# Linear attention feeding a two-layer block: q times k^T v for two chunks at once, with k^T v as the stationary operand

## The chip, the core and the metric

The kernel runs on one core of a Trainium2 chip, in one launch. The metric is the device time of that core in microseconds. The kernel before takes 947.47 us (median of 3 runs, 946.95 to 947.53).

## What is computed

Everything is in 32-bit floats. The reference, cut to what matters:

```python
# q, k, v: (8 batches, 8 heads, 576 positions, 64)
kv  = einsum('bhsd,bhse->bhde', k, v)          # one 64x64 matrix for each batch and head
out = einsum('bhsd,bhde->bhse', q, kv)
x   = out / sqrt(mean(out * out, axis=-1) + 1e-06) * g_norm
x   = x.transpose(0, 2, 1, 3).reshape(4608, 512)
h   = x @ w_in                                 # 512 -> 2048
g   = s * max(h, 0)**2 + b
y   = g @ w_out                                # 2048 -> 512
```

The 4608 rows are handled as 36 chunks of 128, four to a unit, so there are nine units, u = 0 to 8. The two large products take most of the time; the kernel computes them with sums and differences of blocks in place of some of the products. The change touches the small part in front of them: q times k^T v, the norm, and the turning of x.

## The kernel before

While a unit runs its large products, the attention of the four chunks of the next unit is woven in as side work. Unit 0 and unit 1 do this between the products with `w_out` (`side_of`, by slots). The later units do it between the products with `w_in` (`sides`, with places (s, n), where s is the block of the hidden size, 0 to 3, and n the place within it):

```python
for s in range(NS if u > 0 else 0):
    a = steps[s]
    at(0);  a["x1"]()
    if s:  x3(steps[s - 1])
    a["z2"]();  at(1)
    if s:  y4(steps[s - 1])
    a["x6"]();  at(2)
    a["y7"]()
    # ... cut
    at(3);  a["x5"]()
```

Each of x1, z2, x6, y7, x5, x3, y4 is four matmuls of 256 columns on the full array, and each 32-bit matmul appears in the profile as two records, so such a product is a row of `x8`.

The attention of a chunk, cut to the form of chunks 4 and later:

```python
def turn():                        # q^T: by VectorE in 32x32 blocks (chunks 9 and later)
    st["qT"] = attp.tile([P, NP, P], FP32, name="qT", tag="qT")
    nc.vector.transpose(out=st["qT"], in_=q_in[c])      # earlier chunks: TensorE, then a copy

def product():                     # q^T stationary in 128x32 tiles, k^T v moves
    pool, tag = (ps_f, "y") if c > 16 and c % 2 else (ps_a, "x")
    ps = pool.tile([P, NP, P], FP32, name="x_ps", tag=tag)
    for w in range(4):
        for p in range(NP):        # NP = 4: pairs of heads
            nc.tensor.matmul(ps[32 * p : 32 * p + 32, w, :],
                lhsT=st["qT"][:, p, 32 * w : 32 * w + 32],
                rhs=bd_kv[(b if w < 2 else b1) % 2][:, p, :], start=True, stop=True)
    nc.scalar.activation(st["xn"], st["x"], AF.Square)
# row_sum: VectorE sums; norm: ScalarE root, VectorE reciprocal and scaling;
# turn_x: VectorE turns x in 32x32 blocks, ScalarE scales by g_norm
```

`bd_kv[b % 2]` holds k^T v of batch b, two heads of a pair as the diagonal blocks of a 128x128 matrix. `kv_product(b)` makes it, and it is due in the unit before the first chunk that needs batch b:

```python
kv_due = {(b // 2 * R + b % 2 * 4) // 4 - 1: b for b in range(2, B)}   # {1: 2, 2: 3, 3: 4, ...}
```

In unit 2, `kv_product(3)` stands at (1, 3). Its k and v come through the same ring of seven buffers and the same SyncE queue as the weights (`pump`). In unit 1 that queue also loads q for the first two chunks of unit 3, in eight parts between the pumps (`loads_in_parts(3, 0, 8)` at slots 6 to 13). The places of the side work in unit 2 before:

```python
first = {
    (1, 0): [turn[0]],
    (1, 1): [product[0], row_sum[0]],
    (1, 2): [norm[0]],
    (1, 3): [*kv, turn_x[0]],
    (2, 0): [turn[1]],
    (2, 1): [product[1], row_sum[1]],
    (2, 2): [norm[1], *q[0]],
    (2, 3): [turn_x[1], turn[2]],
    (3, 0): [product[2], row_sum[2]],
    # ... cut
}
second = {3: [product[3]], "sums": [row_sum[3]], "norm": [norm[3]], 4: [turn_x[3]]}
```

Of the kernel before, what the change touches and what calls it, by code (L numbers as in the profile page):

```python
# [16 lines left out]
def kernel(  # L17
# [39 lines left out]
    nc = tc.nc  # L57
# [19 lines left out]
    qp = ctx.enter_context(tc.tile_pool(name="qp", bufs=2))  # L77
    attp = ctx.enter_context(tc.tile_pool(name="attp", bufs=2))
    xp = ctx.enter_context(tc.tile_pool(name="xp", bufs=1))
# [13 lines left out]

    kv_in, q_in, w_raw = {}, {}, {}

# [33 lines left out]
    def load_q(c, queues=(nc.sync, nc.sync)):  # L129

        t = qp.tile([P, 2 * DM], FP32, name="q_sb", tag="q")
        pieces = []
        for i in range(2):
# [259 lines left out]

    def attention(c, first=False):

# [3 lines left out]


        b, b1 = parts(c)[0][0], parts(c)[-1][0]
        st = {}

        def turn():
            st["qT"] = attp.tile([P, NP, P], FP32, name="qT", tag="qT")
            if c >= R:
                nc.vector.transpose(out=st["qT"], in_=q_in[c])
                return  # L410
            if c in (0, 2):
                ps = ps_a.tile([P, NP, P], FP32, name="qT_ps", tag="x")
            elif c == 3:
                ps = bank_of("q", "z", 1).rearrange("p b (m n) -> p (b m) n", m=2)
            else:
                ps = ps_t.tile([P, NP, P], FP32, name="qT_ps", tag="t")
            for p in range(NP):
                nc.tensor.transpose(ps[:, p, :], q_in[c][:, 2 * p : 2 * p + 2, :], ident)
            st["q_ps"] = ps
            if not first:  # L420
                take()

        def take():
            if first and c != 1:
                nc.vector.tensor_copy(out=st["qT"], in_=st["q_ps"])
            else:
                nc.scalar.copy(st["qT"], st["q_ps"])

        def product(with_sum=True):
            if first:  # L430
                ps = bank_of("att", "xy"[c % 2]).rearrange("p b (m n) -> p (b m) n", m=2)
            else:
                pool, tag = (ps_f, "y") if c > 16 and c % 2 else (ps_a, "x")
                ps = pool.tile([P, NP, P], FP32, name="x_ps", tag=tag)
            if c < 2:
                for p in range(NP):
                    matmul(ps[:, p, :], st["qT"][:, p, :], bd_kv[0][:, p, :], True, True)
            for w in range(4 if c >= 2 else 0):
                for p in range(NP):
                    nc.tensor.matmul(  # L440
                        ps[32 * p : 32 * p + 32, w, :],
                        lhsT=st["qT"][:, p, 32 * w : 32 * w + 32],
                        rhs=bd_kv[(b if w < 2 else b1) % 2][:, p, :],
                        start=True,
                        stop=True,
                    )
            st["x"] = ps.rearrange("p c (l d) -> p (c l) d", l=2)
            st["xn"] = attp.tile([P, H, D], FP32, name="xn", tag="xn")
            nc.scalar.activation(st["xn"], st["x"], AF.Square)
            if with_sum:  # L450
                row_sum()

        def row_sum():
            st["ss"] = attp.tile([P, H], FP32, name="ss", tag="ss")
            nc.vector.reduce_sum(st["ss"], st["xn"], axis=mybir.AxisListType.X)

        def norm():
            rms = attp.tile([P, H], FP32, name="rms", tag="rms")
            nc.scalar.activation(rms, st["ss"], AF.Sqrt, bias=eps_col, scale=1.0 / D)
            inv = attp.tile([P, H], FP32, name="inv", tag="inv")  # L460
            nc.vector.reciprocal(inv, rms)
# [10 lines left out]
        def turn_x():  # L472
            u, j = divmod(c, 4)
            if j == 0:
                pool = late["x"] if u > 2 and u % 2 else xp
                xT[u] = pool.tile([P, KC, 2 * TB], FP32, name="xT", tag="xT")
            to = xT[u][:, :, j * P : j * P + P]
# [13 lines left out]
            if j % 2 == 1:  # L491
                to = xT[u][:, :, j * P - P : j * P + P]
                for i in range(KC):
                    nc.scalar.activation(  # L494
                        to[:, i], to[:, i], AF.Copy, scale=g_col[:, i : i + 1]
                    )

        return turn, product, norm, turn_x, take, row_sum

    def whole(product, norm):  # L500
        def run():
            product()
            norm()
        return run

# [664 lines left out]

    turn, product, norm, turn_x, take, _ = zip(*(attention(c, True) for c in range(4)))
    slots0 = [slot for s in range(NS) for slot in mm1_plain(s)]
# [37 lines left out]

    def chunks_of(u):
        return list(zip(*(attention(c) for c in range(4 * u, 4 * u + 4))))

    def side_of(u):

        turn, product, norm, turn_x, *_ = chunks_of(u + 1)
        product = [whole(*steps) for steps in zip(product, norm)]
        side = {
            2: [turn[0]],
            3: [product[0]],  # L1220
            4: [turn[1]],
            5: [turn_x[0], product[1]],
            6: [turn[2]],
            7: [turn_x[1], product[2]],
            8: [turn[3]],
            9: [turn_x[2], product[3]],
            11: [turn_x[3]],
            12: [lambda: [sums() for sums in x_sums(u + 1)]],
        }
        if u == 0:  # L1230
            side = {
                6: [lambda: kv_product(1)],
                7: [turn[0]],
                8: [product[0], turn[1]],
                9: [turn_x[0], product[1], turn[2]],
                10: [turn_x[1], product[2], turn[3]],
                11: [turn_x[2], product[3]],
                12: [turn_x[3], lambda: [sums() for sums in sums_w_in(0)]],
                13: side[12],
            }  # L1240
        if u == 1:
            for n, fn in enumerate(loads_in_parts(3, 0, 8)):
                side.setdefault(6 + n, []).append(fn)
# [44 lines left out]
    def sides(u):  # L1288
# [4 lines left out]
        if u + 1 < U:  # L1293
            turn, product, norm, turn_x, _, row_sum = chunks_of(u + 1)
            product = [partial(fn, False) for fn in product]
        kv = [lambda: kv_product(kv_due[u]), lambda: pump(NP)] if u in kv_due else []
# [6 lines left out]
        if u + 1 == U:  # L1303
            return first, second
        if u == 2:
            first = {
                (1, 0): [turn[0]],
                (1, 1): [product[0], row_sum[0]],
                (1, 2): [norm[0]],
                (1, 3): [*kv, turn_x[0]],  # L1310
                (2, 0): [turn[1]],
                (2, 1): [product[1], row_sum[1]],
                (2, 2): [norm[1], *q[0]],
                (2, 3): [turn_x[1], turn[2]],
                (3, 0): [product[2], row_sum[2]],
                (3, 1): [norm[2]],
                (3, 2): [turn_x[2]],
                (3, 3): [turn[3]],
            }
            second = {3: [product[3]], "sums": [row_sum[3]], "norm": [norm[3]], 4: [turn_x[3]]}  # L1320
            for n, fn in enumerate(loads_in_parts(4, 1, 3)):
                second["q", n] = [fn]
        else:
            first = {
                (0, 1): [turn[0]],
                (0, 3): [turn[1]],
                (1, 1): product[:2],
                (1, 2): row_sum[:2],
                (1, 3): [*kv, *q[0], *norm[:2]],
                (2, 0): turn_x[:2],  # L1330
            }
            if u > 3:
                first[1, 2] = [*turn[2:], *row_sum[:2]]
                first[2, 0] = [*turn_x[:2], *q[1]]
                first.update({
                    (2, 1): product[2:],
                    (2, 2): row_sum[2:],
                    (2, 3): norm[2:],
                    (3, 0): [turn_x[2]],
                    (3, 1): [turn_x[3]],  # L1340
                })
            else:
                first[2, 0] = [*turn_x[:2], turn[2]]
                parts = loads_in_parts(5, 1, 4)
                second["q", 0] = [parts[3]]
                first.update({
                    (2, 1): [product[2]],
                    (2, 2): [turn[3], row_sum[2], norm[2], *parts[:3]],
                    (2, 3): [turn_x[2]],
                    (3, 0): [product[3], row_sum[3]],  # L1350
                    (3, 1): [norm[3]],
                    (3, 2): [turn_x[3]],
                })
        second[5], second[6] = [[lambda n=n: x_sums(u + 1)[n]()] for n in range(2)]
# [93 lines left out]
```

## Time and profile before

| what | value |
|---|---|
| time, median of 3 | 947.47 us |
| span of the profiled execution | 945.3 us |
| TensorE matmul busy | 931.7 us, 99% |
| VectorE busy | 657.1 us, 70% |
| ScalarE busy | 205.0 us, 22% |
| DMA | 165.85 MB, mean 175 GB/s |
| products of q with k^T v (line 440) | 1056 + 32 records |

In the profile PE is TensorE, PEld its loading of the stationary operand, DVE VectorE, ACT ScalarE, POOL GpSimd and SP SyncE. L440 is line 440 of the kernel. In a timeline a row gives its start, its length, engine, line, operation, `written<-read`, the form, and `xN` records merged into it; a bracket at the end is idle time before it and what ended that. A busy TensorE is not TensorE at its peak, since records overlap: what a stretch costs is read from the starts of the rows around it. A wait for several things is put down to the one that came last.

### The profile page before, as it was taken

Reading aid. Unit: us, or ns where it says so; the run is one execution under the profiler, and the core shown is the slowest. Engines: PE = TensorE matmul, PEld = TensorE weight load, DVE = VectorE, ACT = ScalarE, POOL = GpSimd, SP = SyncE. Lnnn points to the kernel's source line nnn. Section 1 sums busy time; section 2 is a strip of 40 time slices with the busy share of each in tenths; the row PEclk is TensorE's granted clock in tenths of the full one; section 3 lists DMA queues with packets and bytes.
Section 4 is the critical chain, followed back from the end, with each engine's and each line's share of the span. In section 5 each row is a group of like instructions: output and inputs, shape, how many; then the busy total and the mean of one; then the engine's idle time right before and its main releaser. Section 6 shows DMA issues by size and latency. Waiting matters only on the chain.

```text
span 945.3 us, 18302 instructions
## 1 busy us (share of the span) xinstructions
PE 931.7 (99%) x7438; PEld 841.4 (89%) x7438; DVE 657.1 (70%) x1220; ACT 205.0 (22%) x387; POOL 87.8 (9%) x170
## 2 busy tenths in 40 slices
PE   7999999999999999999999999999999999999997
PEld 7888888888888998899889988999889988998997
DVE  2789767576567785777577756786678757774585
ACT  2784131111122012310232013201320033001200
POOL 2000011033500020000200030003000200021000
PEclk9999999999999999999999999999999999999999
DMA  9688827468952676257544864378326800681075
GB/s 231 211 314 248 266 79 218 118 208 273 286 161 65 221 231 194 36 180 224 193 112 131 262 196 111 78 248 267 98 46 220 304 16 12 204 291 52 12 233 168
DMA packets 129571, 165.85 MB, mean 175 GB/s; under 512 B 78160, under 2 KB 85072, under 8 KB 129360
## 3 DMA queue, kind: packets, MB, share of 16 engines
q1 hardware_dynamic: 118256, 142.71, 49.7%
q0 software_dynamic: 7488, 19.41, 6.2%
q10 hardware_dynamic: 3744, 2.56, 1.1%
q8 instruction: 59, 0.97, 0.4%
q14 instruction: 24, 0.20, 0.1%
HBM read 136.84 MB, written 27.79 MB: 174 GB/s over the span
## 4 chain that ended last, share of the span: by engine, by line
PE 65%; DVE 2%; ACT 1%; issue 0%
PE x_ps L91 27%; PE y_ps L91 18%; PE t_ps L91 8%; PE z_ps L91 8%; PE x_ps L440 2%; PE kv_ps L377 1%; ACT xT L494 1%; DVE a L637 0%; DVE s L247 0%; DVE a L250 0%; DVE a L551 0%; DVE xT L488 0%; DVE a L247 0%; ACT a L631 0%; ACT r L596 0%
## 5 line engine op out<-in xcount | busy, mean ns | idle before, releaser
L596 ACT COPY r<-x_ps 128x512 f32<-128x512 f32 x96 | 56.0, 584 | 397.5 <-PE x_ps L91 375.9
L91 PE MATMUL y_ps<-xs,wb 128*128 128x256 f32 x512 | 122.7, 382 | 0.3 <-DVE a L247 0.3
L91 PE MATMUL x_ps<-xs,ws 128*128 128x256 f32 x512 | 122.0, 381 | 0.5
L822 POOL DMA_DIRECT2D out_dram<-o x110 | 54.5, 502 | 696.7 <-DVE o L247 537.8
L91 PEld LDWEIGHTS x_ps<-xs,ws 128*128 128x128 f32 x512 | 96.4, 190 | 15.3 <-ACT r L596 2.3
L91 PEld LDWEIGHTS y_ps<-xs,wb 128*128 128x128 f32 x512 | 95.4, 190 | 16.3 <-DVE a L247 2.5
L247 DVE TENSOR_TENSOR a<-y_ps,r 128x512 f32<-128x512 f32 x64 | 43.8, 684 | 76.9 <-ACT r L596 59.9
L91 PE MATMUL x_ps<-xT,wa 128*128 128x256 f32 x384 | 89.8, 380 | 0.1
L91 PEld LDWEIGHTS x_ps<-xT,wa 128*128 128x128 f32 x384 | 72.2, 190 | 10.5 <-ACT xT L494 0.5
L91 PE MATMUL y_ps<-w_sb,sub 128*128 128x128 f32 x560 | 69.5, 275 | 0.1
L91 PEld LDWEIGHTS y_ps<-w_sb,sub 128*128 128x128 f32 x560 | 66.4, 192 | 0.6 <-DVE sub L250 0.3
L551 DVE SCALAR_TENSOR_TENSOR a<-a 128x512 f32<-128x512 f32 x89 | 61.5, 691 | 2.8
L91 PE MATMUL y_ps<-w_sb,a 128*128 128x128 f32 (+1 forms) x416 | 61.1, 295 | 0.0
L91 PE MATMUL x_ps<-xT,ws 128*128 128x256 f32 x256 | 60.5, 379 | 0.0
L91 PE MATMUL z_ps<-xT,wa 128*128 128x256 f32 x256 | 60.5, 379 | 0.0
L91 PE MATMUL x_ps<-w_sb,s 128*128 128x256 f32 x256 | 57.8, 380 | 0.0
L91 PEld LDWEIGHTS y_ps<-w_sb,a 128*128 128x128 f32 x416 | 55.4, 192 | 2.2 <-issue 0.2
L91 PE MATMUL t_ps<-w_sb,sub 128*128 128x128 f32 x448 | 54.8, 275 | 0.0
L91 PEld LDWEIGHTS z_ps<-xT,wa 128*128 128x128 f32 x256 | 48.6, 190 | 6.6
L91 PEld LDWEIGHTS x_ps<-xT,ws 128*128 128x128 f32 x256 | 48.1, 190 | 6.3
L91 PEld LDWEIGHTS x_ps<-w_sb,s 128*128 128x128 f32 x256 | 47.5, 190 | 6.0 <-issue 0.2
L91 PEld LDWEIGHTS t_ps<-w_sb,sub 128*128 128x128 f32 x448 | 52.3, 192 | 0.2
(146 smaller groups left out, 1379.1 us busy)
## 6 DMA issues: line engine op xcount, KB each, us to landing
w_sb<-w SPq DMA_DIRECT2D x154, 512.0 KB, 4.7
w_sb<-w SPq DMA_DIRECT2D x42, 256.0 KB, 3.5
w_raw<-in_moe_w_in_dram SPq DMA_DIRECT2D x8, 1024.0 KB, 7.3
w_raw<-in_moe_w_out_dram SPq DMA_DIRECT2D x8, 1024.0 KB, 4.9
w_sb<-in_k_dram SPq DMA_DIRECT2D x48, 144.0 KB, 3.3
w_sb<-in_v_dram SPq DMA_DIRECT2D x48, 144.0 KB, 3.8
w<-sub POOLq DMA_DIRECT2D x24, 256.0 KB, 5.2
out_dram<-o POOLq DMA_DIRECT2D x92, 64.0 KB, 3.9
```

The source lines that it names most:

```text
L91: nc.tensor.matmul(o, lhsT=lhsT, rhs=rhs, start=start, stop=stop, skip_group_check=True)
L247: nc.vector.tensor_tensor(out=o, in0=a, in1=b, op=ALU.add)
L377: nc.tensor.matmul(ps[r][l * HB : l * HB + HB, i, :], lhsT=kv[l][rows, 0, j, :], rhs=kv[l][rows, 1, j, :], start=(j == 0), stop=(j == R - 1),)
L440: nc.tensor.matmul(ps[32 * p : 32 * p + 32, w, :], lhsT=st["qT"][:, p, 32 * w : 32 * w + 32], rhs=bd_kv[(b if w < 2 else b1) % 2][:, p, :] ...
L494: nc.scalar.activation(to[:, i], to[:, i], AF.Copy, scale=g_col[:, i : i + 1])
L551: nc.vector.scalar_tensor_tensor(t, t, 0.0, t, ALU.max, ALU.mult)
L596: nc.scalar.copy(st[name], src)
L822: queues[s % 2].dma_start(out=view[b, jj, :, cols], in_=st[name, j][s * w : s * w + w, cols])
```

## The change

From chunk 4 on, two chunks (256 rows of x) are handled together. k^T v becomes the stationary operand, in tiles of 64 rows by 32 columns, and q^T moves past it, 256 columns in one matmul. This swaps the roles of the operands: fewer stationary loads, longer moves, and eight tiles in place of four. The result arrives turned, so VectorE turns it back in 32x32 blocks, out of PSUM into the tile that held q. Where the 256 rows belong to two batches, the columns are split in two runs. The norm's steps work on both chunks at once.

```diff
-    attp = ctx.enter_context(tc.tile_pool(name="attp", bufs=2))
+    attp = ctx.enter_context(tc.tile_pool(name="attp", bufs=1))
...
+    def attention_of_two(c):
+        ...
+        def turn(i=None):          # one VectorE transpose of both chunks' q
+            ...
+        def product():
+            ps = [ps_t.tile([P, 2, 2 * P], FP32, name="y_ps", tag="t") for _ in range(2)]
+            for b, lo, hi in runs:
+                for r in range(2):
+                    for p in range(NP):
+                        for l in range(2):
+                            rows = slice(l * HB, l * HB + HB)
+                            at = l * HB + r * 32
+                            nc.tensor.matmul(
+                                ps[l][32 * p : 32 * p + 32, r, lo:hi],
+                                lhsT=bd_kv[b % 2][rows, p, at : at + 32],
+                                rhs=st["qT"][rows, p, lo:hi],
+                                start=True, stop=True)
+            st["y"] = q_tile[c].rearrange("p (w l d) -> p w l d", w=W, l=2)
+            for l in range(2):
+                nc.vector.transpose(
+                    out=st["y"][:, :, l].rearrange("p w (r e) -> p r w e", r=2),
+                    in_=ps[l].rearrange("p r (w t) -> p r w t", w=W))
+        def square():   # ScalarE, 1024 elements out of SBUF
+        def row_sum():  # VectorE sum, ScalarE root
+        def norm():     # VectorE reciprocal and scaling
+        def turn_x():   # VectorE
```

The places change as well. All of `first` and `second` for units 2 to 7 is replaced by one list (A is the pair of the first two chunks, B that of the others):

```diff
+        soon = u == 2
+        first = {
+            (0, 1): [A["turn"], *(kv if soon else [])],
+            (0, 3): [A["product"]],
+            (1, 0): [A["square"]],
+            (1, 1): [*([] if soon else kv), A["row_sum"]],
+            (1, 2): [A["norm"], B["turn"]],
+            (1, 3): q[0],
+            (2, 0): [A["turn_x"], A["scale"]],
+            (2, 1): [B["product"]],
+            (2, 2): [B["square"]],
+            (2, 3): [B["row_sum"]],
+            (3, 0): [B["norm"]],
+            (3, 1): [B["turn_x"], *q[1]],
+            (3, 2): [B["scale"]],
+        }
```

In units 0 and 1 the four chunks' steps in `side_of` become two pairs' steps at slots 2 to 12. Loads and `pump` keep their places in unit 1; in unit 2 and later all q loads stand at (1, 3) and (3, 1).

More of the change, by code (lines that the diff above doesn't have):

```diff
@@ L91, in matmul @@
         nc.tensor.matmul(o, lhsT=lhsT, rhs=rhs, start=start, stop=stop, skip_group_check=True)
-    kv_in, q_in, w_raw = {}, {}, {}
+    kv_in, q_in, q_tile, w_raw = {}, {}, {}, {}
     def load_kv(b, i, pool, queues=(nc.sync, nc.sync), **kw):
@@ L133, in load_q @@
         t = qp.tile([P, 2 * DM], FP32, name="q_sb", tag="q")
+        q_tile[c] = t
         pieces = []
@@ L394, with half_of, small, attention @@
     late, xT = {}, {}
-    def attention(c, first=False):
-        b, b1 = parts(c)[0][0], parts(c)[-1][0]
+    two_of = {}
+    def half_of(name, c):
+        if c % 2 == 0:
+            two_of[name] = attp.tile([P, 2 * DM], FP32, name=name, tag=name)
+        t = two_of[name]
+        if name == "qT":
+            return t.rearrange("p (a x) -> p a x", a=NP)[:, :, c % 2 * P : c % 2 * P + P]
+        return t[:, c % 2 * DM : c % 2 * DM + DM].rearrange("p (h d) -> p h d", h=H)
+    def small(name, n, i=""):
+        return attp.tile([P, n], FP32, name=name, tag=f"{name}{i}")
+    def attention(c):
         st = {}
         def turn():
[L407 to L410, printed above, removed]
+            st["qT"] = half_of("qT", c)
             if c in (0, 2):
@@ L419, in turn @@
             st["q_ps"] = ps
-            if not first:
-                take()
         def take():
-            if first and c != 1:
+            if c != 1:
                 nc.vector.tensor_copy(out=st["qT"], in_=st["q_ps"])
@@ L427, in take @@
                 nc.scalar.copy(st["qT"], st["q_ps"])
[L429 to L434, printed above, removed]
+        def product():
+            ps = bank_of("att", "xy"[c % 2]).rearrange("p b (m n) -> p (b m) n", m=2)
             if c < 2:
@@ L442, in product @@
                         lhsT=st["qT"][:, p, 32 * w : 32 * w + 32],
-                        rhs=bd_kv[(b if w < 2 else b1) % 2][:, p, :],
+                        rhs=bd_kv[0][:, p, :],
                         start=True,
@@ L447, in product @@
             st["x"] = ps.rearrange("p c (l d) -> p (c l) d", l=2)
-            st["xn"] = attp.tile([P, H, D], FP32, name="xn", tag="xn")
+            st["xn"] = half_of("xn", c)
             nc.scalar.activation(st["xn"], st["x"], AF.Square)
[L450 to L454, printed above, removed]
+            st["ss"] = small("ss", H, c % 2)
             nc.vector.reduce_sum(st["ss"], st["xn"], axis=mybir.AxisListType.X)
         def norm():
-            rms = attp.tile([P, H], FP32, name="rms", tag="rms")
+            rms = small("rms", H, c % 2)
             nc.scalar.activation(rms, st["ss"], AF.Sqrt, bias=eps_col, scale=1.0 / D)
-            inv = attp.tile([P, H], FP32, name="inv", tag="inv")
+            inv = small("inv", H, c % 2)
             nc.vector.reciprocal(inv, rms)
@@ L474, in turn_x @@
             if j == 0:
-                pool = late["x"] if u > 2 and u % 2 else xp
-                xT[u] = pool.tile([P, KC, 2 * TB], FP32, name="xT", tag="xT")
+                xT[u] = xp.tile([P, KC, 2 * TB], FP32, name="xT", tag="xT")
             to = xT[u][:, :, j * P : j * P + P]
@@ L491, in turn_x @@
             if j % 2 == 1:
[L492 to L504, printed above, removed]
+                scale_x(u, j - 1)
+        return turn, product, norm, turn_x, take
@@ new lines, in scale_x @@
+    def scale_x(u, j):
+        to = xT[u][:, :, j * P : j * P + 2 * P]
+        for i in range(KC):
+            nc.scalar.activation(to[:, i], to[:, i], AF.Copy, scale=g_col[:, i : i + 1])
+    def attention_of_two(c):
+        u, j = divmod(c, 4)
+        by_block = []
+        for i in range(2):
+            p = parts(c + i)
+            by_block += [p[0][0]] * 2 + [p[-1][0]] * 2
+        runs = []
+        for w, b in enumerate(by_block):
+            if runs and runs[-1][0] == b:
+                runs[-1][2] = 32 * w + 32
+            else:
+                runs.append([b, 32 * w, 32 * w + 32])
+        W = 8
+        st = {}
+        def turn(i=None):
+            if i in (None, 0):
+                st["qT"] = attp.tile([P, 2 * DM], FP32, name="qT", tag="qT").rearrange(
+                    "p (a x) -> p a x", a=NP
+                )
+            if i is None:
+                nc.vector.transpose(
+                    out=st["qT"], in_=q_tile[c].rearrange("p (a x) -> p a x", a=NP)
+                )
+                return
+            to = st["qT"][:, :, i * P : i * P + P]
+            if c + i >= R:
+                nc.vector.transpose(out=to, in_=q_in[c + i])
+                return
+            ps = ps_t.tile([P, NP, P], FP32, name="qT_ps", tag="t")
+            for p in range(NP):
+                nc.tensor.transpose(ps[:, p, :], q_in[c + i][:, 2 * p : 2 * p + 2, :], ident)
+            nc.scalar.copy(to, ps)
+        def product():
+            ps = [ps_t.tile([P, 2, 2 * P], FP32, name="y_ps", tag="t") for _ in range(2)]
+            for b, lo, hi in runs:
+                for r in range(2):
+                    for p in range(NP):
+                        for l in range(2):
[5 more added lines that the diff above has]
+                                rhs=st["qT"][rows, p, lo:hi],
+                                start=True,
+                                stop=True,
+                            )
+            st["y"] = q_tile[c].rearrange("p (w l d) -> p w l d", w=W, l=2)
+            for l in range(2):
+                nc.vector.transpose(
+                    out=st["y"][:, :, l].rearrange("p w (r e) -> p r w e", r=2),
+                    in_=ps[l].rearrange("p r (w t) -> p r w t", w=W),
+                )
+        def square():
+            st["xn"] = attp.tile([P, 2 * DM], FP32, name="xn", tag="xn")
+            nc.scalar.activation(st["xn"], q_tile[c], AF.Square)
+        def row_sum():
+            st["ss"] = small("ss", 2 * W, 2)
+            nc.vector.reduce_sum(
+                st["ss"], st["xn"].rearrange("p (h d) -> p h d", d=D), axis=mybir.AxisListType.X
+            )
+            st["rms"] = small("rms", 2 * W, 2)
+            nc.scalar.activation(st["rms"], st["ss"], AF.Sqrt, bias=eps_col, scale=1.0 / D)
+        def norm():
+            inv = small("inv", 2 * W, 2)
+            nc.vector.reciprocal(inv, st["rms"])
+            shape = (P, 2 * W, KC, D // KC)
+            nc.vector.tensor_tensor(
+                out=st["xn"].rearrange("p (c h e) -> p h c e", c=KC, h=2 * W),
+                in0=q_tile[c].rearrange("p (h c e) -> p h c e", h=2 * W, c=KC),
+                in1=inv.unsqueeze(2).unsqueeze(3).to_broadcast(shape),
+                op=ALU.mult,
+            )
+        def turn_x():
+            if j == 0:
+                pool = late["x"] if u > 2 and u % 2 else xp
+                xT[u] = pool.tile([P, KC, 2 * TB], FP32, name="xT", tag="xT")
+            nc.vector.transpose(
+                out=xT[u][:, :, j * P : j * P + 2 * P],
+                in_=st["xn"].rearrange("p (c x) -> p c x", c=KC),
+            )
+        return dict(
+            turn=turn, product=product, square=square, row_sum=row_sum, norm=norm,
+            turn_x=turn_x, scale=lambda: scale_x(u, j),
+        )
@@ L1168 @@
     gp = ctx.enter_context(tc.tile_pool(name="gp", bufs=NS // 2))
-    turn, product, norm, turn_x, take, _ = zip(*(attention(c, True) for c in range(4)))
+    turn, product, norm, turn_x, take = zip(*(attention(c) for c in range(4)))
     slots0 = [slot for s in range(NS) for slot in mm1_plain(s)]
@@ L1209, with pairs_of @@
         step(2)
-    def chunks_of(u):
-        return list(zip(*(attention(c) for c in range(4 * u, 4 * u + 4))))
+    def pairs_of(u):
+        return [attention_of_two(c) for c in (4 * u, 4 * u + 2)]
     def side_of(u):
[L1216 to L1229, printed above, removed]
+        A, B = pairs_of(u + 1)
+        sums = lambda: [fn() for fn in x_sums(u + 1)]
         if u == 0:
@@ L1232, in side_of @@
                 6: [lambda: kv_product(1)],
[L1233 to L1239, printed above, removed]
-            }
-        if u == 1:
+                7: [partial(A["turn"], 0), partial(A["turn"], 1)],
+                8: [A["product"], A["square"]],
+                9: [A["row_sum"], partial(B["turn"], 0), partial(B["turn"], 1)],
+                10: [A["norm"], A["turn_x"], A["scale"], B["product"], B["square"]],
+                11: [B["row_sum"], B["norm"]],
+                12: [B["turn_x"], B["scale"], lambda: [fn() for fn in sums_w_in(0)]],
+                13: [sums],
+            }
+        else:
+            side = {
+                2: [partial(A["turn"], 0), partial(A["turn"], 1)],
+                4: [A["product"], A["square"]],
+                5: [A["row_sum"], B["turn"]],
+                6: [A["norm"]],
+                7: [A["turn_x"], A["scale"], B["product"], B["square"]],
+                8: [B["row_sum"]],
+                9: [B["norm"]],
+                11: [B["turn_x"], B["scale"]],
+                12: [sums],
+            }
             for n, fn in enumerate(loads_in_parts(3, 0, 8)):
@@ L1293, in sides @@
         if u + 1 < U:
-            turn, product, norm, turn_x, _, row_sum = chunks_of(u + 1)
-            product = [partial(fn, False) for fn in product]
+            A, B = pairs_of(u + 1)
         kv = [lambda: kv_product(kv_due[u]), lambda: pump(NP)] if u in kv_due else []
@@ L1304, in sides @@
             return first, second
[L1305 to L1353, printed above, removed]
@@ new lines, in sides @@
+        soon = u == 2
[13 more added lines that the diff above has]
+            (3, 2): [B["scale"]],
+        }
```

## The prediction

> **What bounds the kernel.** I read the page's shares first, then TensorE's list of waits, then its timeline around the attention.
>
> ```profile
> PE 931.7 (99%) x7438; PEld 841.4 (89%) x7438; DVE 657.1 (70%) x1220; ACT 205.0 (22%) x387; POOL 87.8 (9%) x170
> PEclk9999999999999999999999999999999999999999
> ...
> PE x_ps L440 <- DVE xn L463: 0.5, 1, 0.5
> PE x_ps L440 <- DVE qT L409: 0.5, 1, 0.5
> ```
>
> TensorE never rests, at full clock; its listed waits come to some 7 us, of which these two 0.5 us belong to line 440 (the product that is changed). So the time is what TensorE's stream takes, and a change is worth what it takes out of the stream, less any wait it puts in. The timeline gives the cost of one chunk's product (above the "...") and of two chunks at one place (below):
>
> ```profile
> 258.93 1.89 PE L91 MATMUL z_ps<-xT,wa 128*128 128x256 f32 x8
> 260.75 1.08 PE L440 MATMUL x_ps<-bd_kv,qT 128*32 128x128 f32 x32
> 261.76 1.99 PE L91 MATMUL y_ps<-xs,wb 128*128 128x256 f32 x8
> 263.59 1.89 PE L91 MATMUL x_ps<-xs,ws 128*128 128x256 f32 x8
> ...
> 561.12 1.89 PE L91 MATMUL z_ps<-xT,wa 128*128 128x256 f32 x8
> 562.94 1.95 PE L440 MATMUL x_ps<-bd_kv,qT 128*32 128x128 f32 x64
> 564.82 1.99 PE L91 MATMUL y_ps<-xs,wb 128*128 128x256 f32 x8
> 566.65 1.89 PE L91 MATMUL x_ps<-xs,ws 128*128 128x256 f32 x8
> ```
>
> Undisturbed, rows of x8 start 1.727 us apart. One chunk: 263.59 - 258.93 - 2 x 1.727 = 1.21 us. Two: 566.65 - 561.12 - 2 x 1.727 = 2.08 us. The difference, 0.87 us, is the stream of one chunk; the rest, 0.34 us, is paid once at each place, for changing to small tiles and back. A plain x8 row of 256 columns takes 216 ns a record, so 128 columns would take 108; here a record takes 0.87 / 32 = 27 ns, so four tiles do run side by side.
>
> **What the Trainium skill says.** "TensorEngine Tiling (Array Packing)", Tiling Modes: 64x32 gives eight independent tiles, 128x32 four, and a change of mode drains the array. The trace agrees for four tiles and for the drain (0.34 us a place); eight tiles appear in no trace yet. "VectorE: DVE Perf Modes", The three transpose paths: VectorE turns 32x32 blocks only, which is all the change needs; L409 below is such a turn. "DMA: Bandwidth & Descriptors", Issuing engines are not separate DMA queues: transfers from SyncE and GpSimd share the 16 DMA engines; the trace agrees below. "TensorE: Matmul & The Clock Gate", Part 1: after about 3.4 us idle the clock drops to half, for about as long; no run here shows it yet, PEclk being full throughout.
>
> **The change, part by part.**
>
> *TensorE.* A pair becomes 16 matmuls, 32 records, of 256 columns in eight tiles: 32 x 216 / 8 = 0.86 us, in place of 1.75. With the fixed 0.34: 1.20 us. Six of 16 pairs have two runs (64 records, the same columns); I add 0.05. After: 10 x 1.20 + 6 x 1.25 = 19.5 us. Before, by the timeline, units 0, 1 and 2 place chunks singly, unit 3 places two singly and two together, units 4 to 7 pairs: 14 x 1.21 + 9 x 2.08 = 35.7 us. **Saved 16.2 us.** It also removes: the two 0.5 us waits above; 0.1 us in each of four units where y7 waited for the PSUM bank that a chunk had used; some 0.5 us of side work in the second half of unit 2; and 0.28 us in five units where the last x5 waited behind ScalarE's scaling by g. I count 2.5 us of this. **Sum 18.7 us.**
>
> *VectorE and ScalarE.*
>
> ```profile
> L409 DVE STREAM_TRANSPOSE qT<-q_sb 128x512 f32<-128x512 f32 x27 | 17.9, 690 | 0.0
> L455 DVE TENSOR_REDUCE ss<-xn 128x8 f32<-128x512 f32 x36 | 23.5, 674 | 10.5 <-ACT xn L449 10.4
> L227 ACT ACTIVATE w_raw<-w_raw 128x1024 uint32<-128x1024 uint32 x15 | 17.5, 1168 | 0.0
> ```
>
> A pair adds two turns out of PSUM, 2 x 0.69 = 1.4 us. Merging four steps (turn, sum, scaling, turn of x) into 1024 elements saves some 0.15 us each, judging by L409, 0.69 us for 512 elements, of which about 0.53 at one element a cycle; the second reciprocal goes too, 0.2. Net +0.6 us a pair, 10 us in all, on an engine with 288 us free. The squares go from 2 x 0.596 us to one of about 1.17 (L227). Off the path.
>
> *The places.* This is where I expect the loss. The changed program's order has kv_product(3) in unit 2 right after x1 and z2, and A's product two products later. Before, it stood at 267.14:
>
> ```profile
> 248.57 1.89 PE L91 MATMUL z_ps<-xT,wa 128*128 128x256 f32 x8
> 267.14 1.04 PE L377 MATMUL kv_ps<-w_sb 64*64 64x64 f32 x56
> ...
> 253.79 2.75 SPq L115 DMA_DIRECT2D w_sb<-in_k_dram  x2
> 256.58 1.24 SPq L115 DMA_DIRECT2D w_sb<-in_v_dram  x2
> 264.62 1.84 SPq L1261 DMA_DIRECT2D q_sb<-in_q_dram  x4
> ...
> w_sb<-in_v_dram SPq DMA_DIRECT2D x2, 144.0 KB, 3.7
> ...
> q_sb<-in_q_dram SPq DMA_DIRECT2D x4, 8.0 KB, 4.1
> ...
> 240.00:250.00 10.00, 10.00 (x48) 8.81 (x47) 6.97 (x12) 2.29 (x5) 7.16 (x13) 1.00 1.01 336
> ```
>
> The SyncE rows are the last k and v for batch 3, and the last q of the first two chunks of unit 3; the two rows below them, from the DMA view of those issues, give the median from issue to landing. The last row has DMA's share as last but one: full. So v is there at about 256.9 + 3.7 = 260.6, the last q at about 265.6 + 4.1 = 269.7. At 267.14 the first was no wait; chunk 13, which alone uses the last pieces of q, was turned at 273.8. The SyncE queue of the changed program has the same order up to here, so these landings come earlier only as far as unit 1 itself does. By unit 2's start TensorE has gained 2 x 2.9 = 5.8 us (four singles, 4.84 us, and a 0.5 us wait, for two pairs, 2.4, in each of units 0 and 1); I let the landings gain 5.2, the DMA engines being full. Then:
> - unit 2 starts at 246.84 - 5.8 = 241.0; the first half of kv_product(3) is done at 241.0 + 3.45 + 0.1 + 1.25 = 245.8;
> - its second half waits for v, 260.6 - 5.2 = 255.4: **9.6 us**; it is done at 256.7, x6 and y7 at 260.2;
> - VectorE turns both chunks' q in one instruction, so it needs all of it: 269.7 - 5.2 = 264.5, plus 1.25 for the turn and 0.1: A's product starts at 265.9, **5.7 us** more.
>
> Together 15.3 us idle. The clock may halve in the first wait, but kv's second half, x6 and y7 would then eat into the second wait, not add to the sum. Later units: kv at (1, 1) is some 15 us into the unit, and its data lands 7 to 11 us in (issues of batch 5, 6 and 7); no wait.
>
> Total: 947.5 - 18.7 + 15.3 = 944.1.
>
> **The rivals.**
> 1. *No wait for data.* If the loads gained much more than TensorE, all 18.7 us stay: 929. Against it: the queue's order is unchanged, and the DMA engines are full in that stretch.
> 2. *Eight tiles don't run side by side.* Then a pair takes 1.75 + 0.34 as before, the saving is 35.7 - 16 x 2.08 = 2.4 plus 2.5, and with the waits the time is about 957. For it: no trace shows eight. Against it: kv_product's 64x64 tiles split rows and columns too, and at 144 records in about 2.5 us, 17 ns a record, they are issued faster than the 27 ns needed here.
> 3. *VectorE becomes the bound in the first half of a unit.* Per block it has 9 steps of 0.69 = 6.2 us for 12.1 us of TensorE; a pair adds at most 4.2 us to one block. 10.4 of 12.1 fits, but late copies could cost 1 or 2 us a unit: 950.
> 4. *q's tile now serves until the norm*, so the next load of q starts later and may hold up weights in the same queue. Loads stand after the norm in every unit, and the weights run seven buffers ahead; I give it 1 us.
>
> **Range and chances.** The gain is firm to about 2 us if eight tiles hold, the idle time to about 4: 937 to 951. Faster by over 2% needs under 928.5, which rival 1 with all its gains barely reaches: 0.04. Slower by over 2% needs 966: rivals 2 and 3 together: 0.03.
>
> **What would show it.** Right: in the changed profile the pair's row has x32 (or two rows) and costs 1.2 us by the starts around it; TensorE's waits show kv_ps waiting for DMA about 10 us and the pair's product waiting for VectorE's turn of q about 6 us, both in unit 2 and nowhere else; VectorE's busy time is about 10 us higher. Wrong: if unit 2 starts without those waits, my landings were wrong; if a pair costs 2 us, the tiles were; if small waits appear in every unit, VectorE is.

## The result: slightly slower, 955.7 us

| | us, median | range |
|---|---|---|
| before | 947.5 | 946.95 to 948.75 |
| after | 955.68 | 955.35 to 957.89 |

The ratio of after to before is 1.0081, with a 95% interval of 1.0064 to 1.0098. The prediction was 944 us, 937 to 951; the measured time lies 11.6 us above its centre and outside its range.

The shares and the clock, from the page of the changed kernel:

```profile
PE 922.4 (96%) x7118; PEld 830.4 (87%) x7118; DVE 670.8 (70%) x1175; ACT 197.0 (21%) x355; POOL 87.8 (9%) x170
...
PEclk9999999999799999998999999999999999999999
```

TensorE is busy for 9.3 us less than before and yet ends later. It no longer runs without a rest: its share fell from 99% to 96%, and the clock has two dents, at slices 11 and 19, which are about 240 to 263 us and 430 to 454 us. TensorE's list of waits (what waited, for what, us in total, times, the longest) says what lies there:

```profile
PE kv_ps L378 <- DMA w_sb<-in_v_dram: 10.3, 3, 8.3
PE x_ps L91 <- DMA w_sb<-w: 5.7, 1, 5.7
PE y_ps L547 <- DVE qT L526: 2.6, 1, 2.6
...
PE x_ps L91 <- ACT r L688: 2.2, 6, 0.4
```

The first and the third were predicted. The second, a large product waiting for weights, was not.

The pair itself, in TensorE's timeline of unit 5 (start, length, engine, line, operation, form, records):

```profile
569.74 1.89 PE L91 MATMUL y_ps<-xs,wb 128*128 128x256 f32 x8
571.56 1.09 PE L547 MATMUL y_ps<-qT,bd_kv 64*32 64x256 f32 x32
572.58 1.99 PE L91 MATMUL x_ps<-xs,ws 128*128 128x256 f32 x8
574.41 1.89 PE L91 MATMUL x_ps<-xT,wa 128*128 128x256 f32 x8
```

By the starts around it the pair costs 574.41 - 569.74 - 2 x 1.727 = 1.22 us. A pair with two runs costs 1.29 us where the runs are 128 and 128 columns (the rows around it start at 592.64 and 597.38), and 1.40 us where they are 64 and 192 (494.03 and 498.88, in unit 4).

The units show where the time went. Each number is the time from the start of a unit's first product to that of the next, read from TensorE's timeline:

| unit | 0 | 1 | 2 | 3 | 4 | 5 | 6 | 7 |
|---|---|---|---|---|---|---|---|---|
| before | 115.16 | 105.18 | 101.65 | 100.25 | 100.29 | 100.24 | 100.26 | 97.32 |
| after | 113.13 | 102.56 | 115.24 | 107.58 | 98.60 | 98.61 | 98.60 | 95.91 |

Six units gain 1.4 to 2.6 us each. Unit 2 loses 13.6 and unit 3 loses 7.3.

**Unit 2**, in TensorE's timeline after; a bracket is idle time ahead of a row and what ended it:

```profile
246.67 1.37 PE L378 MATMUL kv_ps<-w_sb 64*64 64x64 f32 x74
...
257.81 0.47 PE L378 MATMUL kv_ps<-w_sb 64*64 64x64 f32 x2 [8.35 <-DMA w_sb<-in_v_dram]
259.08 2.15 PE L378 MATMUL kv_ps<-w_sb 64*64 64x64 f32 x66 [0.80 <-DMA w_sb<-in_v_dram]
261.16 3.68 PE L91 MATMUL x_ps<-xs,ws 128*128 128x256 f32 x8
...
269.19 1.36 PE L547 MATMUL y_ps<-qT,bd_kv 64*32 64x192 f32 x64 [2.62 <-DVE qT L526]
```

`kv_product(3)` stops half way for v, then A's product waits for the turn of q. In between, x6 takes 3.68 us where a row of x8 takes 1.89: that is half clock (the granted clock is 0.50 from 255 to 264 us).

**Unit 3.** First SyncE's own waits between 360 and 470 us, then its timeline after the longest of them, then TensorE's:

```profile
SPq L1341 <- DVE xn L577: 15.1, 2, 11.5
```

```profile
401.08 23.36 SPq L1341 DMA_DIRECT2D q_sb<-in_q_dram  x48
424.54 0.38 SPq L779 DMA_DIRECT2D w_sb<-w  x1
```

```profile
429.13 6.73 PE L91 MATMUL x_ps<-w_sb,s 128*128 128x256 f32 x16 [5.71 <-DMA w_sb<-w]
```

A load of q stands 11.5 us in SyncE's queue until B's norm (L577) has read the tile it is to fill. When that ends, at 401.1 us, 48 small loads are still to be issued, 23 us in all, some 0.5 us each from start to start. The next weights, behind them in the same queue, go out at 424.54, which is 66.2 us into the unit. The same load and the same row of matmuls before:

```profile
404.00 0.38 SPq L687 DMA_DIRECT2D w_sb<-w  x1
...
415.04 3.62 PE L91 MATMUL x_ps<-w_sb,s 128*128 128x256 f32 x16
```

The weights then went out 55.5 us into the unit (it starts at 348.49), and the row did not wait. After the wait the row of x16 takes 6.73 us where it took 3.62 before: half clock again (granted clock 0.50 from 429 to 435 us).

### The profile page after: what moved, and what is told of

Read it like the earlier page. It is cut to its first block, busy times and chain, and to the rows that moved or that the text cites. A ratio compares the mean times of both kernels' runs of the same rounds, so it can differ in the third digit from the quotient of the medians.

```text
span 956.1 us, 17631 instructions
## 1 busy us (share of the span) xinstructions
PE 922.4 (96%) x7118; PEld 830.4 (87%) x7118; DVE 670.8 (70%) x1175; ACT 197.0 (21%) x355; POOL 87.8 (9%) x170
## 4 chain that ended last, share of the span: by engine, by line
PE 81%; DVE 6%; SPq 6%; DMA 3%; ACT 3%; issue 1%; ACTq 0%; DVEq 0%
PE x_ps L91 36%; PE y_ps L91 25%; PE z_ps L91 9%; PE t_ps L91 8%; SPq L1341 2%; SPq L1352 2%; PE kv_ps L378 2%; DVE a L248 1%; PE y_ps L547 1%; DMA w_raw<-in_moe_w_in_dram 1%; ACT r L688 1%; SPq L115 1%; ACT xT L498 1%; DVE a L643 1%; DMA kv_sb<-in_k_dram 1%
## 5 line engine op out<-in xcount | busy, mean ns | idle before, releaser
L91 PE MATMUL x_ps<-xs,ws 128*128 128x256 f32 x512 | 124.2, 386 | 2.2 <-ACT r L688 2.2
L91 PEld LDWEIGHTS x_ps<-xs,ws 128*128 128x128 f32 x512 | 96.8, 192 | 20.4 <-ACT r L688 4.6
L248 DVE TENSOR_TENSOR a<-y_ps,r 128x512 f32<-128x512 f32 x64 | 43.7, 683 | 59.8 <-ACT r L688 46.5
L91 PE MATMUL x_ps<-w_sb,s 128*128 128x256 f32 x256 | 61.0, 394 | 5.7 <-DMA w_sb<-w 5.7
L91 PEld LDWEIGHTS x_ps<-w_sb,s 128*128 128x128 f32 x256 | 49.6, 199 | 13.0 <-issue 6.3
L91 PEld LDWEIGHTS y_ps<-w_sb,a 128*128 128x128 f32 x416 | 55.5, 192 | 2.0
```

The costliest lines, as they stand in the source:

```text
L91: nc.tensor.matmul(o, lhsT=lhsT, rhs=rhs, start=start, stop=stop, skip_group_check=True)
L248: nc.vector.tensor_tensor(out=o, in0=a, in1=b, op=ALU.add)
```

## The experiments

Theory P is the prediction's own: the product gains what was worked out, and the places in unit 2 take it away. Theory H came after the first runs: q's tile is held until the norm, and that blocks the queue that the weights need. Every ratio is to the kernel before, timed beside it.

### Unit 2's side work moved to where its data has landed (e1_unit2_later)

```diff
+        if u == 2:
+            first = {
+                (1, 3): kv, (2, 0): [A["turn"]], (2, 1): [A["product"]],
+                (2, 2): [A["square"]], (2, 3): [A["row_sum"]],
+                (3, 0): [A["norm"], B["turn"]],
+                (3, 1): [A["turn_x"], A["scale"], *q[0]],
+                (3, 2): [B["product"]], (3, 3): [B["square"]],
+            }
+            # B's other steps, and q's last load in three parts, go to the second half
```

> Edit: the changed kernel, but in unit 2 kv_product(3) is back at (1, 3), A's steps start at (2, 0) and B's last ones lie in the second half; everything else as changed. Theory P (the places are the loss, the new product is sound): unit 2's 115.2 us fall to about 98.7 (101.65 before, less 2.4 for two pairs in place of four singles and about 0.5 for side work), so 955.7 - 16.5 = 939; TensorE's waits lose the 10.3 us for v and the 2.6 us for q's turn; the 5.7 us for w_sb in unit 3 stay. Rival F (the form is the loss: more VectorE work, q's tile held longer): the waits reappear at the new places, 950 or more. Rival D (the DMA engines are full whatever the order): the wait for w_sb moves or grows, 945 to 950.

941.13 us, ratio 0.9931 (0.9909 to 0.9953). The waits for v and for the turn of q are gone; unit 2 takes 100.37 us in place of 115.24, 14.9 us less. The wait for weights in unit 3 stays, at 5.9 us. Unit 2 did not come down to the expected 98.7: a product of its second half now waits 1.5 us for a sum of VectorE (L810), behind B's steps that were moved there. That wait belongs to the new places, so the old ones cost some 16.4 us.

### The last load of q in unit 3 in three parts (e2_unit3_q_parts, e3_both)

```diff
+        if u == 3:
+            first[(3, 1)] = [B["turn_x"]]
+            for n, fn in enumerate(loads_in_parts(5, 1, 3)):
+                second["q", n] = [fn]
```

The second kernel has this and the edit of the first experiment.

> Edit: the changed kernel, but in unit 3 the loads of q for the second pair of unit 5 (48 of them) go out in three parts of 16 in the second half in place of all at (3, 1). Theory P: the weights behind them in SyncE's queue leave in time, the 5.7 us wait of x_ps for w_sb and the half-clock stretch after it go, unit 3 falls from 107.6 to about 98.5: 946.6. Rival F: VectorE or ScalarE lateness is what makes unit 3 long, the time stays at 953 or more. Rival D: the weights land late whatever stands before them, 950 to 953.

> Edit: both of the other two edits, in units 2 and 3, in the changed kernel. Theory P: the two are independent, 955.7 - 16.5 - 9.1 = 930, which is 1.8% under the kernel before: 16 pairs at 1.2 us for 14 single chunks at 1.21 and 9 pairs at 2.08 (16 us), and little else. Rival F or D: clearly above the sum of the two effects, 938 or more.

954.63 us, ratio 1.0069 (1.0042 to 1.0097), and 940.35 us, ratio 0.9921 (0.9899 to 0.9942). Both expectations missed by 8 to 10 us. The totals lie where rival F put them, but not for its reason: unit 3 did fall, to 100.5 us in both, while unit 4 rose from 98.6 to 105.06 and 104.25. VectorE's timeline of the second kernel in unit 4 shows how:

```profile
470.44 1.25 DVE L526 STREAM_TRANSPOSE qT<-q_sb 128x1024 f32<-128x1024 f32 x1 [4.85 <-DMA q_sb<-in_q_dram]
```

B's q, now loaded later, is late for its turn. VectorE's next sum starts only after this turn, at 471.60 us, and its later steps are late with it; TensorE's longest wait for one of ScalarE's copies grew to 2.7 us. At the end of unit 3 weights came 1.5 and 1.7 us late too. The first kernel's timeline of TensorE has one such place in unit 4, again at half clock (granted clock 0.50 from 499 to 502 us):

```profile
498.40 3.52 PE L91 MATMUL x_ps<-xs,ws 128*128 128x256 f32 x8 [2.75 <-ACT r L688]
```

To spread the loads only moves the delay. What was wanted is to let them start earlier.

### The order of the matmuls within a pair (e4_four_in_turn)

From e3_both, the loop over the two heads outermost, so that neighbours use the same four of the eight tiles:

```diff
-                for r in range(2):
-                    for p in range(NP):
-                        for l in range(2):
+                for l in range(2):
+                    for r in range(2):
+                        for p in range(NP):
```

> Edit: as the run with both edits, but the loop over the two heads of a pair (the two row groups) is outermost in the product, so that four tiles of one row group follow each other, twice, before the other row group's turn; same matmuls, same data. Theory P (TensorE starts matmuls in program order, so eight tiles run together only if eight neighbours differ): a pair costs 1.2 + 0.87 = 2.1 us, 16 x 0.87 = 14 us more than the run with both edits, 944. Rival (the array picks what is free, the order doesn't matter): 930, as without this edit.

941.07 us, ratio 0.994 (0.9915 to 0.9965), against 940.35 for e3_both, with intervals that overlap. The two expected times start from 930 for e3_both, which it missed, so they can't be compared with the time itself; it was their difference, 14 us, that was to be seen, and it isn't there. By the starts around it in TensorE's timeline a pair costs 1.25 us against 1.23. The order is no condition for the eight tiles.

### q's tile set free by the turn (e6_q_tile_free_early)

From e1_unit2_later: for units 3 and later, y is turned back into the tile of q^T, which is no longer needed after the product, and not into q's. So q's tile is free once q is turned, and its next load can stand at (2, 0) in place of (3, 1).

```diff
-            st["y"] = q_tile[c].rearrange("p (w l d) -> p w l d", w=W, l=2)
+            st["yt"] = q_tile[c] if c < 12 else st["qT_tile"]
+            st["y"] = st["yt"].rearrange("p (w l d) -> p w l d", w=W, l=2)
...
+        if u > 2:
+            first[(2, 0)] = [*first[(2, 0)], *q[1]]
+            first[(3, 1)] = [B["turn_x"]]
```

> Edit: the run with unit 2's steps later, and in addition VectorE turns the result back into the tile of q^T, not into that of q (chunks 12 and later), so q's tile is free after its turn as in the kernel before; the loads of q for the second pair go out at (2, 0) in units 3 and later. Theory H (q's tile, held until the norm, keeps SyncE's queue waiting, and 48 small loads then stand in front of the weights): the 11.5 us wait of the queue for the norm goes, no weight is late in unit 3, and nothing is pushed into unit 4 as it was by loading in parts; unit 3 from 107.3 to about 98.5, total 941.1 - 8.8 = 932. Rival D (the small loads delay the weights wherever they stand): unit 3 or 4 stays above 103, total 937 or more.

932.50 us, ratio 0.9846 (0.9827 to 0.9865): as expected. SyncE's timeline in unit 3:

```profile
369.29 26.12 SPq L1341 DMA_DIRECT2D q_sb<-in_q_dram  x51
395.50 0.38 SPq L779 DMA_DIRECT2D w_sb<-w  x1
```

The small loads now pass at 0.5 us each with no stop, and the weights go out 53.9 us into the unit, earlier than before the change (55.5). Unit 3 takes 98.60 us and unit 4 98.66. Against e1_unit2_later this is 8.6 us less, and 9.0 us less than after in unit 3 alone. SyncE's waits for the norm are gone in the whole run. The edit takes away the hold and moves the load in one, so neither was tried alone. But the small loads still stand ahead of the weights here and do no harm, and in e2_unit3_q_parts the tile was held as long, its loads stood behind these weights, and the 5.7 us wait was gone. It took the hold and the loads together. Of TensorE's waits in the later units one remains:

```profile
PE x_ps L91 <- ACT r L688: 1.8, 5, 0.4
PE t_ps L91 <- DVE r L810: 1.5, 1, 1.5
```

The second is the one that the first experiment put into unit 2. The first was in the changed kernel too.

### B one place later (e8_free_early_b_later), and with four tiles (e9_four_tiles)

The first kernel tries to take that remaining wait away: from e6_q_tile_free_early, B's product at (2, 2) and its later steps one place later each. The second does the first's pair over all 128 rows of the pair of heads, where the other head's 64 rows are zero in these columns. That makes four tiles of 128x32, at the same number of matmuls and columns.

```diff
+            first.update({(2, 1): [], (2, 2): [B["product"]], (2, 3): [B["square"]],
+                (3, 0): [B["row_sum"]], (3, 1): [B["norm"]],
+                (3, 2): [B["turn_x"]], (3, 3): [B["scale"]]})
...
-                            rows = slice(l * HB, l * HB + HB)
+                            rows = slice(0, P)      # the second kernel alone
```

> Edit: as the run with q's tile free early, and in units 3 and later B's product stands after y4 and x6, at (2, 2), so that its two turns out of PSUM queue on VectorE behind y4's sum, not ahead of it; B's other steps move one place on. Theory V (the 0.2 to 0.4 us that x5 waits for ScalarE's copy r in each of five units comes from y4's sum, which frees the copy's buffer, being late behind those turns): these waits go, 1.5 us less, 930.5. Rival: the waits come from ScalarE's own load and stay, 932.

> Edit: as the run with B's product later, but every small matmul contracts over all 128 rows (k^T v's other head is zero there), so it uses four tiles of 128x32, not eight of 64x32; the same result and the same number of records. The order of the loop had no effect, so this asks whether eight tiles are used at all. Theory P (eight run side by side): without them a pair costs 1.75 + 0.34 = 2.1 us in place of 1.2, 16 x 0.87 = 14 us more, 944.5. Rival (the array runs four at a time in any case): no change, 930.5.

The first: 936.63 us, ratio 0.9884 (0.9864 to 0.9905), 4.1 us worse than its base instead of better. One wait grew and a new one came, once in each of units 3 to 7:

```profile
PE y_ps L91 <- DVE a L248: 2.7, 5, 0.5
PE x_ps L91 <- ACT r L688: 2.5, 5, 0.6
```

The second: 951.01 us, ratio 1.0025 (1.0003 to 1.0047). The expected time was built on a base of 930.5; what it was to tell, the distance to its base, is 951.01 - 936.63 = 14.4 us, as expected (14 us). TensorE's timeline:

```profile
555.41 1.89 PE L91 MATMUL y_ps<-xs,wb 128*128 128x256 f32 x8
557.23 1.97 PE L546 MATMUL y_ps<-qT,bd_kv 128*32 128x256 f32 x32
...
560.96 1.89 PE L91 MATMUL x_ps<-xT,wa 128*128 128x256 f32 x8
```

A pair costs 560.96 - 555.41 - 2 x 1.727 = 2.10 us with four tiles and 1.22 with eight; 16 x 0.88 = 14.1 us. So eight tiles do run side by side, which is what "TensorEngine Tiling (Array Packing)", Tiling Modes, states. The 0.88 us is half the stream of four tiles, and 1.22 - 0.88 leaves 0.34 us for the place.

### The kernel before, with kv_product(3) at its new place alone (e7_old_kv_early)

```diff
             first = {
+                (0, 1): kv,
...
-                (1, 3): [*kv, turn_x[0]],
+                (1, 3): [turn_x[0]],
```

> Edit: the kernel before, with nothing of the new product; only kv_product(3) in unit 2 is moved from (1, 3) to (0, 1), where the changed kernel has it. Theory P (place alone): TensorE waits there for the last v, some 10 us (it lands about 260.7, the product comes at 250.3), plus 1 to 2 us at half clock: 957 to 959. Rival (the wait belongs to the new form and its other timing): 947 to 949.

961.29 us, ratio 1.0146 (1.0115 to 1.0176): 13 us lost without any of the new product, some 2 us more than expected. TensorE's timeline:

```profile
261.11 2.67 PE L377 MATMUL kv_ps<-w_sb 64*64 64x64 f32 x68 [8.49 <-DMA w_sb<-in_v_dram]
```

The wait is nearly the same (8.35 us in the changed kernel). Unit 2 takes 112.25 us where it took 101.65, and x6 after it 2.77 us in place of 1.89. So 10.6 us are lost at this place; 1.4 us more are lost in unit 3, where a product waits 1.2 us for a sum of VectorE (L718), and 0.8 us ahead of the first product.

### The turns out of PSUM behind the sum of y4 (e10_turn_after_sum)

From e6_q_tile_free_early, in units 3 and later. In the changed kernel the wait for the copy r comes about so: B's two turns out of PSUM stand ahead of VectorE's sum for y4 (they start at 392.56 us, the sum at 393.79), ScalarE's copy, which needs a buffer that this sum frees, starts at 394.53, and x5 waits 0.43 us for it. Here B's matmuls stay at (2, 1), but its turns go to (2, 2). In unit 2 B's steps are spread anew.

```diff
-    (3, 2): [B["product"]], (3, 3): [B["square"]],                     # unit 2
+    (3, 2): [B["product"], B["square"]], (3, 3): [B["row_sum"]],
...
+            first[(2, 1)] = [B["mm"]]                                  # units 3 and later
+            first[(2, 2)] = [B["turn_y"], B["square"]]
```

> Edit: as the run with q's tile free early, with two moves of VectorE work and none of matmuls in units 3 and later: B's matmuls stay at (2, 1), but the two turns out of PSUM are issued at (2, 2), behind y4's sum; in unit 2 B's sum, norm and turn of x move so that no turn of x stands in front of the second half's first copies out of the t bank. Theory V (y4's sum late behind the two turns is what x5 waits for): the 1.8 us that x_ps waits for the copy r goes, and the 1.5 us of t_ps in unit 2 too: 932.5 - 3.3 = 929. Rival S (ScalarE's own queue is what makes the copy late): the 1.8 us stay, 931. In the earlier try the whole product was moved, which shifted B's last steps into the unit's end.

931.59 us, ratio 0.9830 (0.9817 to 0.9844). The wait for r falls from 1.8 to 0.4 us in all, and a unit takes 98.40 us in place of 98.60, so the chain was read rightly. The total alone would fit rival S as well (931); the wait decides between them. In unit 2 the wait of 1.5 us was only exchanged for one of 1.7 us (y_ps waiting for VectorE's sum, L248), and the unit takes 101.19 us in place of 100.46, which is why 929 wasn't reached. It is the lowest time of all, clearly below both kernels; its interval overlaps that of e6_q_tile_free_early, so these two are not told apart.

## Why the prediction was wrong

The step that failed is rival 4: its mechanism was right, but it was sized at 1 us, left out of the sum, and cost 9.0. Three terms of the sum were mis-sized by less: the pairs with two runs, the side waits, and the idle time of unit 2. With the measured terms, from the units' times, the sum is 947.5 - 15.5 + 16.4 + 9.0 = 957.4; the profiled execution took 957.89 us, the median is 955.68. The 15.5 us are what the change gains where nothing is lost: 12.7 in units 0, 1 and 3 to 7 (unit 3 as in e6_q_tile_free_early) and 2.8 in unit 2 (as in e1_unit2_later, without its wait of 1.5 us). The 16.4 us are unit 2's places, the 9.0 us unit 3. This sum only sorts what the traces show and is no test of its own; e6_q_tile_free_early, where both losses are gone, gains 15.6 us by the medians, 12.8 to 16.4 by its ratio.

- **The pair on TensorE: right but for the pairs with two runs.** A pair of one run costs 1.22 us, where 1.20 was predicted. Six pairs have two runs, 1.25 predicted; going by those of units 4 to 6, two cost 1.29 and four 1.40. That is 0.9 us too little in all, and the saving on TensorE is 35.7 - 20.4 = 15.3 us. Rival 2, whose own sum comes to 957.9 us and not to about 957, is ruled out by e9_four_tiles.
- **The side waits: mis-sized, 2.3 of the 3.2 us between 18.7 and 15.5.** Of the 2.5 us next to nothing came (15.5 against 15.3). The 0.28 us where x5 waited (in four units; in unit 3 it was less) did not go: with ScalarE's scaling moved, VectorE's turns out of PSUM took its place (1.8 us in five times from unit 3 on). The two waits of 0.5 us did go, but a wait of 0.5 us for VectorE came in unit 0. In units 5 and 6 the gain is 1.63 and 1.66 us, about what the product alone brings (2 x 2.08 less two pairs, 1.65 and 1.54).
- **VectorE: right in kind.** Busy 13.7 us more, not 10, and off the path for nearly all of it. The turn out of PSUM lasts 691 ns, as assumed:

```profile
L556 DVE STREAM_TRANSPOSE q_sb<-y_ps 128x512 f32<-128x512 f32 x32 | 20.9, 691 | 11.0 <-PE y_ps L547 11.0
```

  Rival 3 was to cost 1 or 2 us a unit. The wait for r behind the turns is 0.4 us a unit, and e10_turn_after_sum gets 0.2 of it back.
- **Unit 2's idle time: near in sum, by two errors that almost cancel.** 15.3 us were predicted and the places cost some 16.4; the waits for v come to 10.3 us (9.6 predicted). But the landings did not gain 5.2 us. SyncE's timeline after, to be set beside that of before in the prediction:

```profile
254.97 1.23 SPq L115 DMA_DIRECT2D w_sb<-in_v_dram  x2
...
262.80 1.84 SPq L1352 DMA_DIRECT2D q_sb<-in_q_dram  x4
```

  Both go out 1.6 to 1.8 us earlier than before. Unit 2 gained too little as well: it starts at 243.13, not 241.0. Of this 0.94 us is a later start of the first product, which differs from run to run (25.1 to 27.4 us over the profiles), and 1.15 is what units 0 and 1 gained less than counted (4.65 of 5.8). Both ends slid by much the same, so their distance nearly held. The halved clock ate into the second wait, as foreseen: 2.62 us of it are left, and x6 took 1.79 us longer.
- **Rival 4: right mechanism, wrong size.** "I give it 1 us" stood on the weights running seven buffers ahead. What it cost is 9.0 us: 5.71 us of waiting and 3.1 us more for a row at half clock. The lead was judged by the number of buffers. It should have been reckoned in time on SyncE's queue: 11.5 us until the norm, then 23 us of small loads, ahead of the weights in order. Before, these weights went out 11.0 us ahead of their row (404.00 and 415.04), and such a load lands 4.7 us after its issue (median); that leaves a lead of some 6.3 us, an estimate, and the change sent them out 10.7 us later in the unit. Unit 3 is the only one hurt. It issues 64 small loads of q, units 4 to 6 issue 48, 48 and 32, and the time that the loads take to issue goes with their number. The queue waits for the norm in later units too (77.4 us in ten times over the whole run, the longest 12.4), without harm. That the fewer loads are what saves the later units was not tried by itself.
- **Rival 1** is out: the data was waited for. "No wait in later units" failed with rival 4.

## What to carry to other kernels

A buffer that is kept alive longer delays not only its own next load but everything behind that load in the same queue: reckon the hold and the issue time of what follows in microseconds against the lead of the tightest load behind it. When side work becomes cheaper and its places are redrawn, compare each place with the landing of its data; here the product was worth some 15.5 us, and the places in unit 2 and the held tile took 25.4. And when a wait is spread out and not removed, look for it in the next unit.

## What the runs showed of the hardware beyond this

- Half clock after idle time adds to the cost of a wait. After 8.35 us idle x6 lasted 3.68 us in place of 1.89, and after 5.71 us idle the row of x16 lasted 6.73 us in place of 3.62. "TensorE: Matmul & The Clock Gate", Part 1, gives about 3.4 us as the idle time that halves the clock. In e2_unit3_q_parts 2.75 us of idle time were followed by 0.50 for some 3.4 us, while the 2.62 us ahead of A's product left the clock at full; so here the limit lies lower, or depends on more than the length of one gap.
- The eight tiles ask for no order of issue: 1.25 us with neighbours in the same four tiles, 1.23 us with neighbours in different ones.
- A small load of q (8 to 32 KB) holds SyncE's queue for 0.43 us (median of the 64 in unit 3, least 0.31); with the gaps between them, 51 of them took 26.1 us in e6_q_tile_free_early.
